# Chunkwise retention with a running K^T V state, plain fp32 loads and an instruction order written by hand, in a retention + gated FFN kernel

## The chip, the cores and the metric

The kernel runs on one core of a Trainium2 chip. The metric is the device time of one execution in microseconds (us), lower is better. TensorE (PE) multiplies matrices, PEld is its weight load, VectorE (DVE), ScalarE (ACT) and GpSimd (POOL) compute elementwise, SyncE (SP) issues DMAs. TensorE writes to PSUM, from which the others copy to SBUF.

## The reference

Retention is attention without softmax: scores are scaled, masked to the causal triangle and weighted by gamma^(i-j), one gamma per head. Its output goes through a sigmoid-gated FFN.

```python
batch, n_heads, seq, head_dim = (8, 8, 576, 64)
scores = scale * np.matmul(q, k.transpose(0, 1, 3, 2))
gamma = 1.0 - 2.0 ** (-5.0 - np.arange(H, dtype=np.float32))
Dmat = np.where(rel >= 0, gamma[:, None, None] ** rel[None, :, :], 0.0)
ret = np.matmul(scores * Dmat[None, :, :, :], v)
# x: ret as (4608 tokens, 512)
gate = 1.0 / (1.0 + np.exp(-(x @ w_gate)))     # w_gate, w_val: 512 x 1536
out = (gate * (x @ w_val)) @ w_out             # w_out: 1536 x 512
```

All inputs and the output are fp32 in memory; both kernels multiply in bf16. Since gamma^(i-j) = gamma^i gamma^(-j), both put one factor into q and the other into k.

## The kernel before

The work has two stages per batch. `attention_batch(b)` makes the 576 tokens of batch b for all eight heads, handled in four pairs of two heads (2 x 64 = 128 partitions). `ffn_window(w)` takes 512 tokens of the result, which lies transposed in `xT`, through the FFN. The main loop issues the loads of the next batch, then attention, then one FFN window; a ninth window ends the program.

Loads (`load_qkv`, lines 119 to 136, and `load_weights`, lines 103 and 106) are all issued by GpSimd and cast fp32 to bf16 on the way. They share eight completion semaphores in turn, so at most eight are on the way. The code asks for batch 0, then all weights, then batch 1. V goes into `vpad`, which holds each head's 64 columns in a 128-wide block of zeros, so that two heads accumulate into one 128-partition result.

Attention, by line:
- 149: transposes of Q and K, 40 a batch, into the PSUM tile `tr` (one buffer).
- 165, 168, 171: VectorE multiplies by the gamma tables on the way out to `qTpad` (zeros in the other head's half) and `kTp`.
- 192, 210: K^T Q for the causal blocks of the full 576 x 576 matrix, 12 matmuls a pair of heads, up to 512 columns wide, into `qk` (three PSUM banks) and `pv`.
- 221 to 235: five masked diagonal blocks on VectorE and four plain copies on whichever engine the framework picks, into `pt`.
- 241 to 262: the products with V, in two parts through one PSUM bank `pv` (one buffer), copied to `xT`.

The FFN window: 12 column blocks, each four matmuls with `wg_sb` (271) and four with `wv_sb` (280), a sigmoid on ScalarE (288) and a product on VectorE (290); then for four blocks of 128 tokens twelve matmuls with `wo_sb` (295), a copy (303) and a store from SyncE (305). Three PSUM buffers `ffn` serve all of it. The order on each engine is set by the framework's scheduler from these loops; it mixes attention of the next batch with the start of a window.

Of the kernel before, what the change touches and what calls it, by code (L numbers as in the profile page):

```python
# [9 lines left out]
FP32 = mybir.dt.float32  # L10
BF16 = mybir.dt.bfloat16
# [5 lines left out]
def kernel(  # L17
# [9 lines left out]
):  # L27
    nc = tc.nc
# [4 lines left out]
    P = 128  # L33

    NPAIR = H // 2
    NSC = (S + P - 1) // P
    SC_OFF = [0, 128, 256, 384, S - P]
    NJC = NSC
    JTAIL = (NSC - 1) * P
    WTAIL = S - JTAIL  # L40
    SPAD = S + WTAIL
    NKC = DM // P
    NFC = DFF // P
    scale = 1.0 / math.sqrt(D)

    consts = ctx.enter_context(tc.tile_pool(name="consts", bufs=1))
    wpool = ctx.enter_context(tc.tile_pool(name="wpool", bufs=1))
    bfpool = ctx.enter_context(tc.tile_pool(name="bfpool", bufs=2))
    pt_pool = ctx.enter_context(tc.tile_pool(name="pt", bufs=4))
    xt_pool = ctx.enter_context(tc.tile_pool(name="xt", bufs=1))  # L50
    gv_pool = ctx.enter_context(tc.tile_pool(name="gv", bufs=13))
# [3 lines left out]
    qk_psum = ctx.enter_context(tc.tile_pool(name="qk_psum", bufs=3, space=bass.MemoryType.PSUM))  # L55
    pv_psum = ctx.enter_context(tc.tile_pool(name="pv_psum", bufs=1, space=bass.MemoryType.PSUM))
    tr_psum = ctx.enter_context(tc.tile_pool(name="tr_psum", bufs=1, space=bass.MemoryType.PSUM))
    ffn_psum = ctx.enter_context(tc.tile_pool(name="ffn_psum", bufs=3, space=bass.MemoryType.PSUM))

    ident = consts.tile([P, P], BF16)  # L60
    make_identity(nc, ident)

    maskfull = consts.tile([P, S], BF16)
    nc.gpsimd.memset(maskfull, 1.0)
    nc.gpsimd.affine_select(
        out=maskfull, in_=maskfull, compare_op=ALU.is_ge, fill=0.0, base=0,
        pattern=[[1, S]], channel_multiplier=-1)

    srow_f = consts.tile([P, S], FP32)
    nc.gpsimd.iota(srow_f, pattern=[[1, S]], base=0, channel_multiplier=0,  # L70
                   allow_small_or_imprecise_dtypes=True)
    grq = consts.tile([P, H, S], BF16)
    gmk = consts.tile([P, NPAIR, S], BF16)
    ln_scale_bias = consts.tile([P, 1], FP32)
    nc.vector.memset(ln_scale_bias, math.log(scale))
    for h in range(H):
        lg = math.log(1.0 - 2.0 ** (-5.0 - h))
        nc.scalar.activation(out=grq[:, h, :], in_=srow_f, func=AF.Exp,
                             bias=ln_scale_bias, scale=lg)
    for m in range(NPAIR):  # L80
        for hh in range(2):
            lg = math.log(1.0 - 2.0 ** (-5.0 - (2 * m + hh)))
            p0 = hh * 64
            nc.scalar.activation(out=gmk[p0:p0 + 64, m, :],
                                 in_=srow_f[p0:p0 + 64, :],
                                 func=AF.Exp, bias=0.0, scale=-lg)

    qTpad = consts.tile([P, 2, H, S], BF16)
    kTp = consts.tile([P, 2, NPAIR, SPAD], BF16)
    vpad = consts.tile([P, 2, NJC, NPAIR, 2, P], BF16)  # L90
    nc.vector.memset(qTpad, 0.0)
    nc.scalar.memzero(kTp)
    nc.gpsimd.memset(vpad, 0.0)  # L93

    wg_sb = wpool.tile([P, NKC, DFF], BF16)
    wv_sb = wpool.tile([P, NKC, DFF], BF16)
    wo_sb = wpool.tile([P, NFC, DM], BF16)

    def load_weights():
        for (dst, src, nch) in ((wg_sb, moe_w_gate, NKC), (wv_sb, moe_w_val, NKC)):  # L100
            for c in range(nch):
                for p0 in range(0, DFF, 512):
                    nc.gpsimd.dma_start(out=dst[:, c, p0:p0 + 512],
                                        in_=src[c * P:(c + 1) * P, p0:p0 + 512])
        for c in range(NFC):
            nc.gpsimd.dma_start(out=wo_sb[:, c, :],
                                in_=moe_w_out[c * P:(c + 1) * P, :])

    xT = xt_pool.tile([P, NPAIR, NT], BF16)

    def load_qkv(b):
        ph = b % 2
        qb = bfpool.tile([P, NSC, H, D], BF16, tag="qb", name=f"qb{b}")
        kb = bfpool.tile([P, NSC, H, D], BF16, tag="kb", name=f"kb{b}")
        for sc in range(NSC):
            s0 = SC_OFF[sc]
            for (t_ap, dst) in ((q, qb), (k, kb)):
                for hw in range(2):
                    nc.gpsimd.dma_start(  # L119
                        out=dst[:, sc, 4 * hw:4 * hw + 4, :],  # L120
                        in_=t_ap[b, 4 * hw:4 * hw + 4, s0:s0 + P, :]
                        .rearrange("h p d -> p h d"))
        for sc in range(NSC):
            s0 = SC_OFF[sc]
            if sc == NSC - 1:
                nc.gpsimd.dma_start(
                    out=vpad[0:WTAIL, ph, sc, :, 0, 0:D],
                    in_=v[b, 0::2, JTAIL:S, :].rearrange("h p d -> p h d"))
                nc.gpsimd.dma_start(
                    out=vpad[0:WTAIL, ph, sc, :, 1, D:2 * D],  # L130
# [214 lines left out]
```

## Time and profile before

| | |
|---|---|
| median of 3 runs | 475.63 us (475.23 to 477.93) |
| the profiled execution (its span, first to last instruction) | 474.0 us |
| TensorE busy | 413.1 us, 87%, 2,470 matmuls recorded |
| VectorE busy | 212.5 us, 45% |
| ScalarE busy | 191.9 us, 40% |
| GpSimd busy | 206.1 us, 43% (most of it DMA issues) |
| DMA queues | GpSimd's: 127,808 packets; SyncE's: 5,184 |
| mean granted TensorE clock | 0.986 |

Busy time of an engine is the union of its instructions. Matmuls overlap, so their starts tell the pace. Some matmul records are missing (of the FFN's 1,296, the page has 1,255). In rows of stretches the columns are: stretch and length, busy time and count of each engine, granted clock, DMA share, GB/s written. In rows of groups: line, engine, operation, out<-in, count, busy us and mean ns, idle time before and what ended it.

### The profile page before, as it was taken

To read this page: it belongs to the slowest core of one execution; us is meant where nothing else is said; L and a number is where in the kernel's file an instruction comes from. 1 tells how busy PE (TensorE), PEld (TensorE's weight loads), DVE (VectorE), ACT (ScalarE), POOL (GpSimd) and SP (SyncE) were. 2 spreads that over 40 slices of the span, in tenths; PEclk is the share of its full clock that TensorE was granted. 3 is DMA by queue.
4 is the path that set the end of the run, shared out by engine and by line. 5 is a ranking of instruction groups with operands and counts; after the bars stand their busy time and mean duration, and the time that the engine had idled before them with its cause. 6 is when DMAs were issued, how large, how long until landed. Compare 5 with 4: busy or idle time off the path is not lost.

```text
span 474.0 us, 6814 instructions
## 1 busy us (share of the span) xinstructions
PE 413.1 (87%) x2470; PEld 217.1 (46%) x2512; DVE 212.5 (45%) x600; ACT 191.9 (40%) x433; POOL 206.1 (43%) x286
## 2 busy tenths in 40 slices
PE   0375799589999899899989998999899998999996
PEld 0133444355445544464445444644465445444442
DVE  3255241487417641674248333844195308441330
ACT  9225332055325532563246332733264326532331
POOL 9997899999407730575048602960000000000000
PEclk9999899789999999999999999999999999999999
DMA  0999999999719951797059703990200010001002
GB/s 0 78 86 182 190 117 124 138 86 91 46 46 101 72 36 44 83 74 51 22 91 88 51 1 96 90 67 2 89 2 1 0 66 24 2 0 61 30 0 89
DMA packets 133025, 29.81 MB, mean 63 GB/s; under 512 B 123776, under 2 KB 128384, under 8 KB 132992
## 3 DMA queue, kind: packets, MB, share of 16 engines
q0 software_dynamic: 127808, 19.94, 57.2%
q1 hardware_dynamic: 5184, 9.44, 5.2%
q8 instruction: 19, 0.31, 0.3%
q14 instruction: 14, 0.11, 0.1%
HBM read 39.85 MB, written 9.44 MB: 104 GB/s over the span
## 4 chain that ended last, share of the span: by engine, by line
PE 73%; DVE 9%; POOL 7%; ACT 5%; DMA 2%; issue 2%; ACTq 0%; DVEq 0%; POOLq 0%
PE op L295 20%; PE h L280 19%; PE h L271 17%; PE qk L192 6%; PE pv L254 4%; PE pv L241 3%; PE tr L149 3%; DVE qTpad L165 2%; DVE qTpad L168 2%; POOL vpad L93 2%; POOL kb L119 2%; POOL qb L119 1%; DVE kTp L171 1%; DMA wv_sb<-in_moe_w_val_dram 1%; ACT pt L232 1%
## 5 line engine op out<-in xcount | busy, mean ns | idle before, releaser
L290 DVE TENSOR_TENSOR gv<-g,h 128x512 bf16<-128x512 bf16 x108 | 74.2, 687 | 127.8 <-PE h L280 107.7
L280 PE MATMUL h<-xT,wv_sb 128*128 128x512 bf16 x426 | 113.6, 379 | 6.6 <-DMA wv_sb<-in_moe_w_val_dram 3.7
L271 PE MATMUL h<-xT,wg_sb 128*128 128x512 bf16 x405 | 111.8, 380 | 1.5 <-DMA wo_sb<-in_moe_w_out_dram 0.8
L119 POOL DMA_DIRECT2D qb<-in_q_dram x80 | 66.3, 918 | 96.2 <-PE tr L149 96.1
L288 ACT ACTIVATE g<-h 128x512 bf16<-128x512 f32 x108 | 63.7, 598 | 106.4 <-PE h L271 98.4
L295 PE MATMUL op<-wo_sb,gv 128*128 128x512 bf16 x424 | 94.3, 379 | 0.5
L192 PE MATMUL qk<-qTpad,kTp 128*128 128x320 bf16 (+3 forms) x319 | 64.7, 303 | 9.5 <-DVE qTpad L165 6.5
L280 PEld LDWEIGHTS <-wv_sb 128*128 128x128 bf16 x432 | 42.3, 98 | 54.8 <-DMA wv_sb<-in_moe_w_val_dram 4.5
L119 POOL DMA_DIRECT2D kb<-in_k_dram x80 | 66.7, 931 | 0.1
L295 PEld LDWEIGHTS <-gv 128*128 128x128 bf16 x432 | 42.3, 98 | 51.0
L271 PEld LDWEIGHTS <-wg_sb 128*128 128x128 bf16 x432 | 42.3, 98 | 46.1
L165 DVE TENSOR_TENSOR qTpad<-tr,grq 64x512 bf16<-64x512 bf16 (+1 forms) x40 | 15.5, 388 | 95.5 <-PE tr L149 95.4
L303 ACT COPY ob<-op 128x512 f32<-128x512 f32 x36 | 21.1, 585 | 80.2 <-PE op L295 80.2
L149 PE MATMUL tr<-ident,qb 128*128 128x128 bf16 x160 | 20.5, 237 | 31.3 <-DVE kTp L171 16.3
L232 ACT CAST pt<-qk 128x384 bf16<-128x384 f32 x55 | 26.4, 480 | 42.8 <-DVE pt L221 42.6
L192 PEld LDWEIGHTS <-kTp 128*128 128x128 bf16 x320 | 27.5, 100 | 24.5 <-issue 11.8
L133 POOL DMA_DIRECT2D vpad<-in_v_dram x32 | 30.4, 950 | 10.2 <-PE pv L254 10.2
L254 PE MATMUL pv<-pt,vpad 128*128 128x192 bf16 (+1 forms) x320 | 29.2, 238 | 5.2 <-ACT xT L249 3.6
L149 PEld LDWEIGHTS <-qb 128*128 128x128 bf16 x160 | 12.4, 104 | 45.5 <-issue 24.2
L136 POOL DMA_DIRECT2D vpad<-in_v_dram x32 | 30.7, 960 | 0.4 <-PE h L271 0.4
L254 PEld LDWEIGHTS <-vpad 128*128 128x128 bf16 x320 | 25.9, 99 | 10.5 <-issue 8.3
L241 PE MATMUL pv<-pt,vpad 128*128 128x384 bf16 (+2 forms) x192 | 29.5, 277 | 0.9 <-DVE pt L229 0.2
(44 smaller groups left out, 342.3 us busy)
## 6 DMA issues: line engine op xcount, KB each, us to landing
out_dram<-ob SPq DMA_DIRECT2D x36, 256.0 KB, 2.0
qb<-in_q_dram POOLq DMA_DIRECT2D x80, 64.0 KB, 3.2
kb<-in_k_dram POOLq DMA_DIRECT2D x80, 64.0 KB, 3.3
vpad<-in_v_dram POOLq DMA_DIRECT2D x64, 64.0 KB, 3.2
wg_sb<-in_moe_w_gate_dram POOLq DMA_DIRECT2D x12, 128.0 KB, 5.5
wv_sb<-in_moe_w_val_dram POOLq DMA_DIRECT2D x12, 128.0 KB, 4.9
wo_sb<-in_moe_w_out_dram POOLq DMA_DIRECT2D x12, 128.0 KB, 4.9
vpad<-in_v_dram POOLq DMA_DIRECT2D x16, 32.0 KB, 3.0
```

The costliest lines, as they stand in the source:

```text
L119: nc.gpsimd.dma_start(out=dst[:, sc, 4 * hw:4 * hw + 4, :], in_=t_ap[b, 4 * hw:4 * hw + 4, s0:s0 + P, :] .rearrange("h p d -> p h d"))
L136: nc.gpsimd.dma_start(out=vpad[:, ph, sc, :, 1, D:2 * D], in_=v[b, 1::2, s0:s0 + P, :].rearrange("h p d -> p h d"))
L149: nc.tensor.matmul(trp[:, idx, :], lhsT=src[:, sc, 2 * m:2 * m + 2, :], rhs=ident, is_transpose=True, start=(idx == 0), stop=(idx == 2 * N ...
L192: nc.tensor.matmul(bank[:, off:off + wi], lhsT=kTp[:, ph, m, lj:lj + P], rhs=qTpad[:, ph, 2 * m + hh, li:li + wi], start=start, stop=stop,)
L232: nc.any.tensor_copy(out=pt[:, 0, P:512], in_=bks1[hh][:, P:512])
L241: nc.tensor.matmul(pvp[:, jc * P:W1], lhsT=vpad[:, ph, jc, m, hh, :], rhs=pts[hh][:, jc, jc * P:W1], start=(n1 == 0), stop=(n1 == 5),)
L254: nc.tensor.matmul(pvp[:, lo - W1:S - W1], lhsT=vpad[:, ph, jc, m, hh, :], rhs=pts[hh][:, jc, lo:S], start=(n2 == 0), stop=(n2 == 9),)
L271: nc.tensor.matmul(h1, lhsT=wg_sb[:, kc, fc * P:(fc + 1) * P], rhs=xT[:, kc, n0:n0 + 512], start=(kc == 0), stop=(kc == NKC - 1),)
L280: nc.tensor.matmul(h2, lhsT=wv_sb[:, kc, fc * P:(fc + 1) * P], rhs=xT[:, kc, n0:n0 + 512], start=(kc == 0), stop=(kc == NKC - 1),)
L288: nc.scalar.activation(out=g, in_=h1, func=AF.Sigmoid)
L290: nc.vector.tensor_tensor(out=gv, in0=g, in1=h2, op=ALU.mult)
L295: nc.tensor.matmul(opp, lhsT=gvs[fc][:, nb * P:(nb + 1) * P], rhs=wo_sb[:, fc, :], start=(fc == 0), stop=(fc == NFC - 1),)
```

## The change

Attention is rewritten; the FFN keeps its matmuls.

- **Chunks with a state.** Each batch is cut into 5 chunks (four of 128 tokens, one of 64), 40 chunks in all. Within a chunk the causal product is formed in two halves of 64 keys, both heads of a pair at once, with K laid in diagonal blocks (`kbd`) and V too (`vbd`). What earlier chunks contribute comes from a 64 x 64 state K^T V per head, summed in one PSUM tile `st` over the batch, and copied with a mask to bf16 (`sb`) after each chunk.
- **Loads.** Q, K and V come as fp32 by SyncE's queue, one DMA each for a chunk (256 KB as fp32, 256 B per row), six chunks ahead. The gamma factors and casts are made on chip before the transposes (`cast`): in the first five chunks K on VectorE, Q on GpSimd, V on ScalarE; later all on GpSimd. Weights stay on GpSimd's queue, in 9 DMAs of 1 MB (as fp32) instead of 36. They too take the eight completion semaphores in turn, so the ninth waits for the first.
- **Order.** The framework's scheduler is off (`manual_schedule`), so each engine runs in the order of the code. Each chunk has four phases: t (transposes), qk, pv, st. The first four chunks run ahead of the FFN; then phases are laid between the FFN's units, each of four matmuls.
- Output copies and their stores go to ScalarE.

The diff, cut to its core:

```diff
+    ctx.enter_context(tc.manual_schedule())
+    STEPS = [(b, c) for b in range(B) for c in range(NC)]
+    def load(s):
...
+        for nm, src in (("k", k), ("q", q), ("v", v)):
+            t = ld_pool.tile([P, H, D], FP32, tag=nm + "32", name=f"{nm}32_{s}")
+            nc.sync.dma_start(out=t[0:n], in_=src[b, :, t0:t0 + n, :].rearrange("h p d -> p h d"))
...
+    LEAD_LOAD = 6
+    LEAD_CAST = 3
...
+    def load_weights():
+        for f0 in range(0, DFF, 512):
+            for dst, src in ((wg_sb, moe_w_gate), (wv_sb, moe_w_val)):
+                nc.gpsimd.dma_start(
+                    out=dst[:, :, f0:f0 + 512],
+                    in_=src[:, f0:f0 + 512].rearrange("(c p) f -> p c f", p=P))
...
+    def cast(s):
...
+        early = s < NC
+        eng = nc.vector if early else nc.gpsimd
+        eng.tensor_tensor(out=ks[0:n], in0=k32[0:n],
+                          in1=ktab[0:n, c, :].unsqueeze(2).to_broadcast([n, H, D]), op=ALU.mult)
+        nc.gpsimd.tensor_tensor(out=qs[0:n], in0=q32[0:n],
+                                in1=qtab[0:n, c, :].unsqueeze(2).to_broadcast([n, H, D]), op=ALU.mult)
...
+        copy(vn[0:n], v32[0:n])
+        for j in range(n // 64):
+            for hh in range(2):
+                copy(vb[hh * 64:hh * 64 + 64, j, :, hh * 64:hh * 64 + 64],
+                     v32[j * 64:j * 64 + 64, hh::2, :])
...
+    def phase_t(s):
...
+                nc.tensor.matmul(trp[:, i * M + m, 0:n], lhsT=src[0:n, 2 * m:2 * m + 2, :],
+                                 rhs=ident[0:n, 0:n], is_transpose=True,
...
+            nc.vector.tensor_copy(
+                out=kb[p0:p0 + 64, 0:nj, :, p0:p0 + 64].rearrange("p j m t -> p m j t"),
+                in_=trp[p0:p0 + 64, 0:M, 0:n].rearrange("p m (j t) -> p m j t", t=64))
...
+        nc.scalar.copy(out=qT[:, :, 0:n], in_=trp[:, M:2 * M, 0:n])
...
+    def phase_qk(s):
...
+                    nc.tensor.matmul(qkp[:, mm, 0:128], lhsT=kb[:, 0, m, :], rhs=qT[:, m, 0:128],
+                                     start=True, stop=True)
+                    nc.tensor.matmul(qkp[:, mm, 128:192], lhsT=kb[:, 1, m, :], rhs=qT[:, m, 64:128],
+                                     start=True, stop=True)
+                nc.vector.tensor_tensor(out=pt[:, 2 * g:2 * g + 2, :], in0=qkp[:, :, 0:192],
+                                        in1=tri.unsqueeze(1).to_broadcast([P, 2, 192]), op=ALU.mult)
...
+    def phase_pv(s):
...
+            if c > 0:
+                mm.append((state[s - 1][:, m, :], qT[:, m, 0:n], 0, n))
+            if n == P:
+                mm.append((vb[:, 0, m, :], pt[:, m, 0:128], 0, 128))
+                mm.append((vb[:, 1, m, :], pt[:, m, 128:192], 64, 128))
...
+        nc.scalar.copy(out=xT[:, :, t0:t0 + n], in_=pvp[:, :, 0:n])
...
+    def phase_st(s):
...
+            nc.tensor.matmul(stp[:, m, :], lhsT=ks[:, 2 * m:2 * m + 2, :], rhs=vn[:, 2 * m:2 * m + 2, :],
...
+    def phase_sv(s):
...
+        nc.vector.tensor_tensor(out=sb, in0=st_tiles[b],
+                                in1=bdm.unsqueeze(1).to_broadcast([P, M, P]), op=ALU.mult)
...
+    order = [("t", 0), ("qk", 0), ("st", 0)]
+    for s in range(NS):
+        if s + 1 < NS:
+            order.append(("t", s + 1))
+        order.append(("pv", s))
+        if s + 1 < NS:
+            order.append(("qk", s + 1))
+            order.append(("st", s + 1))
...
+        for u, _ in enumerate(ffn_units(t0, n)):
+            want = begin + min(todo, -(-todo * (u + 1) // (nu - 3)))
+            while at < want:
+                run_phase(*order[at])
+                at += 1
...
-    staged = load_qkv(0)
     load_weights()
-    for b in range(B):
-        staged_next = load_qkv(b + 1) if b + 1 < B else None
-        attention_batch(b, staged)
-        staged = staged_next
-        ffn_window(b)
-    ffn_window(B)
```

`run_phase`, at t of chunk s, first issues the load of chunk s + 6 and the casts of chunk s + 2.

How this stands on the engines, at the places that the prediction speaks of. GpSimd's start before, from the constants to the first loads of batch 0 (`qb`, `kb`):

```order
L65 AFFINE_SELECT maskfull<-maskfull 128x576
L70 IOTA srow_f 128x576
L93 MEMSET vpad 128x10240
L119 DMA qb_131<-in_q_dram 128x4x64 x2
L119 DMA kb_132<-in_k_dram 128x4x64 x2
```

GpSimd's start after, from the fifth of the nine weight DMAs (ahead of the first stand the constants and the Q scaling of chunks 0 and 1) to the first chunk that it casts alone, number 5; `qs`, `ks` are scaled Q and K of a chunk, `vn` its V:

```order
L134 DMA wg_sb<-in_moe_w_gate_dram 128x4x512
L134 DMA wv_sb<-in_moe_w_val_dram 128x4x512
L138 DMA wo_sb<-in_moe_w_out_dram 128x4x512 x3
L159 TENSOR_TENSOR qs_214<-q_2_107,qtab 128x512
L159 TENSOR_TENSOR qs_263<-q_3_113,qtab 128x512
L159 TENSOR_TENSOR qs_321<-q_4_119,qtab 64x512
L157 TENSOR_TENSOR ks_382<-k_5_123,ktab 128x512
L159 TENSOR_TENSOR qs_381<-q_5_125,qtab 128x512
L166 CAST vn_383<-v_5_127 128x512
```

The weights have moved ahead of most of the loads' consumers: the Q scaling of chunks 2 to 4 stands behind all nine weight DMAs.

ScalarE's rows before, from the gamma tables to the first copies of scores of batch 0:

```order
L78 ACTIVATE grq<-srow_f,ln_scale_bias 128x576 x8
L84 ACTIVATE gmk<-srow_f 64x576 x8
L232 CAST pt_0_0_291<-qk_0_0_0_292 128x384
L232 CAST pt_0_1_295<-qk_0_0_1_296 128x384
L233 CAST pt_0_0_291<-qk_0_0_0_293 128x64
```

ScalarE's rows after, from the gamma tables to the copies of the transposed Q (`qT`) of the first chunks and of the first result (`pv` to `xT`):

```order
L101 ACTIVATE qtab<-arg,lnscale 128x40
L164 CAST vn_181<-v_0_97 128x512
L164 CAST vbd_151<-v_0_97 64x4x64 x4
L164 CAST vn_191<-v_1_103 128x512
L164 CAST vbd_152<-v_1_103 64x4x64 x4
L164 CAST vn_216<-v_2_109 128x512
L164 CAST vbd_153<-v_2_109 64x4x64 x4
L198 COPY qT_235<-tr_224 128x512
L164 CAST vn_265<-v_3_115 128x512
L164 CAST vbd_154<-v_3_115 64x4x64 x4
L198 COPY qT_284<-tr_273 128x512
L245 CAST xT<-pv_286 128x4x128
```

The copy of chunk 0's Q stands behind the casts of V of chunk 2, that of chunk 1 behind those of chunk 3, and so on.

VectorE's rows before inside an FFN window (`gv` is the gate product; the window is the second):

```order
L290 TENSOR_TENSOR gv_9_1209<-g_9_1207,h_1_9_1202 128x512
L290 TENSOR_TENSOR gv_10_1223<-g_10_1221,h_1_10_1216 128x512
L290 TENSOR_TENSOR gv_11_1237<-g_11_1235,h_1_11_1230 128x512
L165 TENSOR_TENSOR qTpad<-tr_4_1383,grq 64x4x64
L168 TENSOR_TENSOR qTpad<-tr_4_1383,grq 64x4x64
L171 TENSOR_TENSOR kTp<-tr_4_1383,gmk 128x4x64
```

VectorE's rows after inside the first window, chunk 5 between the gate products (`kbd` from the transposes, `pt` the masked scores, `sb` the state):

```order
L315 TENSOR_TENSOR gv_1_513<-g_1_506,h_0_1_508 128x512
L194 COPY kbd_157<-tr_531 64x4x2x64 x2
L315 TENSOR_TENSOR gv_2_566<-g_2_549,h_0_2_561 128x512
L215 TENSOR_TENSOR pt_575<-qk_0_576,tri 128x384
L215 TENSOR_TENSOR pt_575<-qk_1_582,tri 128x384
L315 TENSOR_TENSOR gv_3_593<-g_3_573,h_0_3_588 128x512
L265 TENSOR_TENSOR sb_607<-st_602,bdm 128x512
L315 TENSOR_TENSOR gv_4_614<-g_4_600,h_0_4_609 128x512
```

Attention's work, which stood in a block after the gate products, is now spread between them, at most two operations at a time.

442 lines of the change are left out of this document (202 added, 240 removed).

## The prediction

> **What bounds the kernel now.** I read the busy shares first, then the busy time of stretches of the span, then single rows of the timeline. The page's two lines:
>
> ```profile
> span 474.0 us, 6814 instructions
> PE 413.1 (87%) x2470; PEld 217.1 (46%) x2512; DVE 212.5 (45%) x600; ACT 191.9 (40%) x433; POOL 206.1 (43%) x286
> ```
>
> TensorE is far ahead of the others, but its 87% is made of overlapping matmuls, so the stretches and the spacing of starts say more. The stretches are: before the first transpose, up to the first FFN matmul, first FFN window, second batch, and one settled batch.
>
> ```profile
> 0.00:14.40 14.40, 0.00 (x0) 0.00 (x0) 3.96 (x2) 13.51 (x17) 13.76 (x14) 1.00 0.09 6
> 14.40:41.20 26.80, 17.45 (x109) 9.13 (x111) 14.24 (x49) 7.93 (x23) 25.82 (x40) 1.00 1.33 103
> 41.20:85.00 43.80, 37.23 (x189) 18.37 (x192) 11.73 (x27) 14.52 (x29) 40.01 (x62) 0.96 1.38 152
> 85.00:145.00 60.00, 51.91 (x332) 29.04 (x335) 30.93 (x88) 21.67 (x51) 38.77 (x54) 0.91 0.98 79
> 194.30:243.80 49.50, 46.27 (x295) 24.81 (x298) 24.67 (x73) 20.81 (x51) 22.00 (x30) 1.00 0.67 60
> ```
>
> So 85 us pass before the first FFN window is done, the second batch costs 60 us, and from then on a batch costs 49.5 us. Rows of TensorE in settled batches, in order of time, and two of the chain of waits at the end:
>
> ```profile
> 193.87 0.38 PE L149 MATMUL tr<-ident,qb 128*128 128x128 bf16 x4 [0.61 <-DVE kTp L171]
> 194.09 0.39 PE L149 MATMUL tr<-ident,kb 128*128 128x128 bf16 x4
> 207.23 0.88 PE L254 MATMUL pv<-pt,vpad 128*128 128x192 bf16 x10
> 207.94 0.60 PE L192 MATMUL qk<-qTpad,kTp 128*128 128x320 bf16 x4
> 213.15 1.02 PE L280 MATMUL h<-xT,wv_sb 128*128 128x512 bf16 x4
> 214.01 1.03 PE L271 MATMUL h<-xT,wg_sb 128*128 128x512 bf16 x4
> 243.41 0.38 PE L149 MATMUL tr<-ident,qb 128*128 128x128 bf16 x4 [0.61 <-DVE kTp L171]
> 459.61 10.54 PE op L295 x48
> 470.21 0.58 ACT ob L303
> ```
>
> Starts, not durations, give the price of a matmul. Four of 512 columns take 214.01 - 213.15 = 0.86 us, 0.216 each. Four transposes of 128 columns take 0.22, 0.055 each. That is 0.42 ns a column plus about 1.3 ns. The ten of line 254 (eight of 192 columns, two of 64) take 0.71 us, which that line gives too (0.70), so a matmul of 64 columns costs 0.028 us. The same place of two batches lies 243.41 - 193.87 = 49.54 us apart. The FFN's 144 matmuls are 31.1 us of it. The batch's attention is 152 matmuls over 30,720 columns (counted from the code), 13.1 us. The remaining 5.3 us are waits inside attention, such as the 0.61 us for VectorE in two of these rows. After the last matmul (470.15) the span goes on for 3.8 us: a copy and a store.
>
> **TensorE's new work.** The FFN keeps its 1,296 matmuls: 1,296 x 0.216 = 279.9 us. A chunk of 128 tokens now has 8 transposes, 4 products with K, 4 state updates and 8 products with V or the state, 24 of 128 columns, and 8 of 64: 24 x 0.055 + 8 x 0.028 = 1.54 us. The first chunk of a batch has four fewer of 128 (no state yet), 1.32; the last, 64 tokens wide, has 20 of 64 columns, 0.56. A batch is 1.32 + 3 x 1.54 + 0.56 = 6.5 us instead of 13.1, and eight are 52.1. Chunks 0 to 3 and the transposes of chunk 4 (6.2 us) come before the first FFN matmul, so 45.9 us follow it.
>
> The Trainium skill (TensorE: Matmul & The Clock Gate, section Back-to-back issue gap) says that in a stream of weight load and matmul pairs 128 columns settle at about 81 ns a matmul. The transposes above, each with its own weight load, start 55 ns apart, so the trace disagrees. By the page the 636 such matmuls after the start would add 636 x 0.026 = 17 us.
>
> **Stalls between phases.** The phases t, pv, qk and st of a chunk are laid between FFN units of four matmuls (0.86 us), about two units apart. The cover is thus 1.7 us for what VectorE and ScalarE must do between two phases. Their rows:
>
> ```profile
> L290 DVE TENSOR_TENSOR gv<-g,h 128x512 bf16<-128x512 bf16 x108 | 74.2, 687 | 127.8 <-PE h L280 107.7 <-ACT g L288 19.0 <-PE h L271 1.0
> L288 ACT ACTIVATE g<-h 128x512 bf16<-128x512 f32 x108 | 63.7, 598 | 106.4 <-PE h L271 98.4 <-PE h L280 7.9
> L303 ACT COPY ob<-op 128x512 f32<-128x512 f32 x36 | 21.1, 585 | 80.2 <-PE op L295 80.2
> L227 DVE TENSOR_TENSOR pt<-qk,maskfull 128x192 bf16<-128x192 f32 x64 | 22.2, 348 | 0.0
> L223 DVE TENSOR_TENSOR pt<-qk,maskfull 128x128 bf16<-128x128 f32 x64 | 18.3, 286 | 0.8 <-PE qk L192 0.4
> L165 DVE TENSOR_TENSOR qTpad<-tr,grq 64x512 bf16<-64x512 bf16 x32 | 13.3, 415 | 80.0 <-PE tr L149 79.9
> ```
>
> The new mask multiply has 384 columns: from 286 and 348 ns about 1 ns a column, so 534 ns, two per chunk. The K copies are like line 165 (2 x 415 ns), the state's multiply like line 290 (687). With 13.5 gate products VectorE has about 21 us of work in a batch's 41.5; ScalarE, with 13.5 sigmoids, 4.5 output copies and nine copies of about 585 ns, about 16, and the output's DMA issue moves to its queue. Neither is a bound, but their order matters. An FFN buffer (three of them) must be free two units after it was filled, 1.73 us; with both mask multiplies ahead in VectorE's queue its product is done after 2 x 0.53 + 0.69 = 1.76 us, plus a handoff. I take 0.2 us lost in each of the 28 full chunks after the start, 5.6 us. The bounds are 0 (settled FFN rows show no gap) and 5.3 us a batch as now, 38 us over the 7.2 batches left.
>
> **Loads and casts.** A load becomes 1,024 packets of 256 B on SyncE's queue, three loads a chunk. GpSimd issues only weights, in 9 large DMAs, and casts from chunk 5 on. Rows (stretches first):
>
> ```profile
> 40.00:45.00 5.00, 3.03 (x26) 1.71 (x23) 3.30 (x13) 3.64 (x11) 2.91 (x7) 1.00 1.23 195
> 45.00:50.00 5.00, 2.88 (x17) 2.24 (x19) 0.75 (x3) 0.50 (x2) 4.38 (x9) 0.74 1.20 189
> 50.00:55.00 5.00, 3.66 (x26) 2.13 (x25) 0.62 (x3) 1.85 (x5) 4.02 (x9) 0.92 1.20 188
> 62.00:63.50 1.50, 1.50 (x9) 0.67 (x8) 0.69 (x1) 0.37 (x2) 1.50 (x4) 1.00 2.04 130
> 242.49 0.33 SPq L305 DMA_DIRECT2D out_dram<-ob  x1
> out_dram<-ob SPq DMA_DIRECT2D x36, 256.0 KB, 2.0
> 33.44 5.58 POOL L103 DMA_DIRECT2D wg_sb<-in_moe_w_gate_dram  x10
> L65 POOL TENSOR_SCALAR_AFFINE_SELECT maskfull<-maskfull 128x576 bf16<-128x576 bf16 x1 | 0.7, 665 | 0.0
> L93 POOL MEMSET vpad<- 128x10240 bf16 x1 | 8.6, 8627 | 0.0
> ```
>
> At 62 us a backlog of 128 B packets moves at 130 GB/s, 1.02 packets a ns: I take 1.0 us a load, since the packet count is the nearest likeness. Upwards, the store's issue on SyncE (0.33 us for 128 packets of 2 KB) would be 2.6 us if it grew with packets. The weights moved at 188 to 195 GB/s of bf16, so their 4.72 MB take about 25 us.
>
> **First FFN matmul.** Chunk 4's transposes stand ahead of it, so 4.5 chunks, 13.5 loads, must land: 13.5 us plus 2 for landing, 16 us alone. The weights join at about 9.5 us (GpSimd first scales Q of chunks 0 and 1, the latter after the fifth load). If all 25 us of them went first, it would be 41. I take the middle, 28. Then V of chunk 4 is cast on ScalarE ahead of older copies (1.2 us), and three chunks follow one another at about 2.5 us (transposes 0.6, copy 0.6, product 0.3, masks 1.1): 9 us. The first FFN matmul is at 37 us, bounds 25 and 50. The lowered clock at a cold start (0.74 and 0.92 in two rows above) costs (0.26 + 0.08) x 5 = 1.7 us.
>
> **The sum.** 37 + 279.9 + 45.9 + 5.6 + 1.7 + 3.8 = 373.9 us. The profiled execution stands 1.6 us under the median of the runs (474.0 and 475.63), so 375.5: I say 376. Of the 100 us saved, 53 come from columns ((13.1 - 6.5) x 8), about 37 from waits (4.5 us a batch, and 10 more in the second batch), and the rest from the first window.
>
> **Rivals.**
> *Waits stay.* Chunks hand over as slowly as now, 5.3 us a batch: 376 + 38 - 6 = 408. For it: one transpose buffer and one for PV remain. Against: hand-laid FFN units lie between all phases.
> *Weight loads show.* A load lasts 98 ns, longer than a short matmul; if the 43 ns beyond 55 were not hidden, 636 x 0.043 = 27 us, 403. The 55 ns spacing speaks against it.
> *Weights hold GpSimd.* The ninth weight DMA waits for the first, and the Q scaling of chunks 2 to 4 is queued behind it. In the row at 33 us ten issues went 0.53 us apart without a wait, so I count no hold. If GpSimd were held until most of the 25 us had moved, under sharing until about 45, the FFN would start at 55: 394.
> *GpSimd becomes the bound, slower than before.* Per chunk it makes two multiplies of 512 columns, one copy of 512 and four of 256. From its two rows (0.84 ns a column, 0.18 us fixed) a copy is 0.61 or 0.40; the multiplies, with two inputs, between that and twice it. So 3.4 to 4.6 us a chunk, against 41.5/4.5 = 9.2 that TensorE leaves. It decides beyond 9.2. The 31.5 chunks after the fourth begin near 38 us, and 43 us follow the last cast, so 12.5 us a chunk reach 475 and 14 make 522. No arithmetic of this form ran there before.
> *Loads become the bound.* Past 41.5/13.5 = 3.1 us a load; at 3.5, 108 loads and the end give about 425.
>
> The Trainium skill (GPSIMD Engine Reference, section 3.1 Elementwise) gives about 2.6 cycles an element at 1.2 GHz for two inputs. As an estimate from that page a multiply is 1.1 us, which leaves the sum as it is; no run here shows it yet.
>
> **How the numbers follow.** Forecast 0.70; waits stay 0.12; weight loads show 0.03; GpSimd held 0.07; GpSimd bound 0.05; loads bound 0.03. The forecast's own ends: start at 25 and no stalls, 376 - 12 - 5.6 = 358; start at 50 and 15 us of stalls, 376 + 13 + 9.4 = 398. The range is 360 to 408: it leaves out a sliver below, half of "waits stay" and the two bounds. A measurement of this kernel can tell about 0.5% from no change. Faster 0.92, the same 0.02 (the bounds at their thresholds), slower 0.06.
>
> **What would show it.** Right: op rows of neighbouring windows about 37 us apart on average (31.1 plus 5.8), transposes still at 0.055 us, no gap over 0.5 us on TensorE past the first window, GpSimd's casts under 5 us a chunk, first FFN matmul between 25 and 50 us. Wrong: TensorE waiting on casts or loads, or gaps at every phase.

## The result and the profile after

The changed kernel takes 389.81 us (median of 4 runs, 387.2 to 389.84), the kernel before 476.4 beside it (4 runs, 475.23 to 477.93): a ratio of 0.8172 with a 95% interval of 0.8142 to 0.8203. The forecast was 376, range 360 to 408. The profiled execution took 389.82 us, its span 388.1. Its first two lines:

```profile
span 388.1 us, 6403 instructions
PE 341.4 (88%) x2403; PEld 186.0 (48%) x2448; DVE 166.7 (43%) x310; ACT 137.9 (36%) x251; POOL 158.2 (41%) x263
```

TensorE is as far ahead as before, with 72 us less busy time. The stretches, cut as in the prediction: the first transposes, up to the first FFN matmul, the first window, the second, a settled one.

```profile
0.00:12.30 12.30, 1.22 (x8) 0.69 (x8) 5.29 (x18) 6.00 (x13) 9.62 (x24) 1.00 1.10 186
12.30:53.10 40.80, 11.95 (x124) 11.32 (x125) 11.01 (x23) 10.27 (x23) 14.93 (x22) 1.00 1.22 201
53.10:81.10 28.00, 27.61 (x192) 14.77 (x196) 15.26 (x28) 11.23 (x19) 18.80 (x31) 1.00 1.19 203
81.10:118.10 37.00, 36.74 (x268) 19.78 (x271) 17.52 (x32) 14.54 (x26) 17.38 (x30) 1.00 0.78 161
155.40:192.40 37.00, 36.68 (x267) 19.76 (x271) 17.55 (x32) 14.44 (x26) 18.18 (x32) 1.00 0.48 118
```

From 53.1 us on TensorE is busy for all but 0.3 to 0.4 us of each window. Nearly all that went other than forecast lies in the second row: 40.8 us, of which TensorE works 12. TensorE's rows at the same place of two neighbouring windows:

```profile
154.99 0.39 PE L187 MATMUL tr<-ident,ks 128*128 128x128 bf16 x4
155.21 0.39 PE L187 MATMUL tr<-ident,qs 128*128 128x128 bf16 x4
155.43 1.03 PE L321 MATMUL op<-wo_sb,gv 128*128 128x512 bf16 x3
...
192.37 0.81 PE L321 MATMUL op<-wo_sb,gv 128*128 128x512 bf16 x3
```

Four transposes still start 0.22 us apart, and the op rows of two neighbouring windows lie 36.94 us apart where one place of two batches lay 49.54 (each has one FFN window; the attention in it is that of 512 tokens now, of 576 before). The engines that copy, by groups:

```profile
L159 POOL TENSOR_TENSOR qs<-q,qtab 128x512 bf16<-128x512 f32 (+1 forms) x40 | 41.7, 1042 | 22.7 <-DMA q<-in_q_dram 22.4
L215 DVE TENSOR_TENSOR pt<-qk,tri 128x384 bf16<-128x384 f32 x64 | 32.7, 552 | 75.5 <-PE qk L213 75.5
L166 POOL CAST vbd<-v 64x256 bf16<-64x256 f32 x126 | 50.2, 399 | 54.8 <-PE pv L244 50.8
L166 POOL CAST vn<-v 128x512 bf16<-128x512 f32 (+1 forms) x35 | 21.3, 608 | 0.6 <-DMA v<-in_v_dram 0.6
L138 POOL DMA_DIRECT2D wo_sb<-in_moe_w_out_dram x3 | 2.3, 775 | 0.7 <-DMA wg_sb<-in_moe_w_gate_dram 0.7
```

**Where the start goes.** The casts of chunks 3 and 4 in order of time, each started by its load, and the steps of TensorE after them (the bracket holds the idle time before and what ended it):

```profile
20.39 0.69 DVE L157 TENSOR_TENSOR ks<-k,ktab 128x512 bf16<-128x512 f32 x1 [1.76 <-DMA k<-in_k_dram]
27.04 1.04 POOL L159 TENSOR_TENSOR qs<-q,qtab 128x512 bf16<-128x512 f32 x1 [8.51 <-DMA q<-in_q_dram]
33.62 0.62 ACT L164 CAST vn<-v 128x512 bf16<-128x512 f32 x1 [17.25 <-DMA v<-in_v_dram]
40.45 1.04 POOL L159 TENSOR_TENSOR qs<-q,qtab 64x512 bf16<-64x512 f32 x1 [12.37 <-DMA q<-in_q_dram]
43.69 0.62 ACT L164 CAST vn<-v 64x512 bf16<-64x512 f32 x1 [6.81 <-DMA v<-in_v_dram]
45.70 0.26 PE L211 MATMUL qk<-qT,kbd 128*128 128x128 bf16 x1 [6.12 <-ACT qT L198]
49.44 0.27 PE L211 MATMUL qk<-qT,kbd 128*128 128x128 bf16 x1 [0.59 <-ACT qT L198]
53.11 0.59 PE L306 MATMUL h<-xT,wg_sb 128*128 128x512 bf16 x1 [0.73 <-ACT xT L245]
```

The three loads of chunk 3 land 6.6 us apart, those of the half-size chunk 4 3.2 us. Before the weights moved it was 1.2 us a load: V of chunks 0, 1 and 2 started its cast at 6.42, 10.05 and 13.59 us, three loads apart. The DMA view of three stretches, 5 to 10, 20 to 25 and 43.2 to 44.5 us (packets, MB, share of 16 engines; q1 is SyncE's queue, q0 GpSimd's), shows why; the last row is the issue of one load on SyncE:

```profile
q1 hardware_dynamic: 4328, 1.09, 138.8%
...
q0 software_dynamic: 776, 0.78, 91.4%
q1 hardware_dynamic: 776, 0.20, 29.8%
...
q1 hardware_dynamic: 1357, 0.34, 132.1%
...
7.29 1.14 SPq L78 DMA_DIRECT2D q<-in_q_dram  x1
```

While both queues have work, they move the same number of packets, though a weight packet holds 1 KB and a load's 256 B. The loads drop from 4,328 packets to 776, a fifth; the weights move at 156 GB/s (0.78 MB in 5 us) where they had 188 to 195 in the kernel before, so they lose only about a fifth. The loads crawl until the last weight is in, at 43.4 us. The 1.2 us of a load without weights may be the pace of SyncE's issues, 1.14 us each: behind the last weight, where loads had queued up, 1,357 packets go in 1.3 us, 1.0 us a load.

### The profile page after: what moved, and what is told of

Its sections match the earlier page's. It is cut to its first block, busy times and chain, and to the rows that moved or that the text cites. A ratio compares the mean times of both kernels' runs of the same rounds, so it can differ in the third digit from the quotient of the medians.

```text
span 388.1 us, 6403 instructions
## 1 busy us (share of the span) xinstructions
PE 341.4 (88%) x2403; PEld 186.0 (48%) x2448; DVE 166.7 (43%) x310; ACT 137.9 (36%) x251; POOL 158.2 (41%) x263
## 4 chain that ended last, share of the span: by engine, by line
PE 85%; SPq 6%; DMA 4%; issue 1%; ACT 1%; DVE 0%; ACTq 0%
PE h L306 48%; PE op L321 24%; SPq L78 6%; PE pv L244 4%; DMA v<-in_v_dram 4%; PE tr L187 4%; PE qk L211 2%; PE st L256 2%; PE qk L213 1%; ACT qT L198 0%; PE qk L220 0%; ACT vbd L164 0%; DVE pt L215 0%; DVE kbd L194 0%; ACT ob L326 0%
## 5 line engine op out<-in xcount | busy, mean ns | idle before, releaser
L166 POOL CAST vbd<-v 64x256 bf16<-64x256 f32 x126 | 50.2, 399 | 54.8 <-PE pv L244 50.8
L157 POOL TENSOR_TENSOR ks<-k,ktab 128x512 bf16<-128x512 f32 (+1 forms) x35 | 36.4, 1041 | 76.1 <-issue 57.9
L215 DVE TENSOR_TENSOR pt<-qk,tri 128x384 bf16<-128x384 f32 x64 | 32.7, 552 | 75.5 <-PE qk L213 75.5
L306 PEld LDWEIGHTS <-wg_sb 128*128 128x128 bf16 x432 | 40.9, 99 | 45.3 <-issue 2.5
L159 POOL TENSOR_TENSOR qs<-q,qtab 128x512 bf16<-128x512 f32 (+1 forms) x40 | 41.7, 1042 | 22.7 <-DMA q<-in_q_dram 22.4
L211 PE MATMUL qk<-qT,kbd 128*128 128x128 bf16 x128 | 16.3, 228 | 32.5 <-ACT qT L198 32.4
L198 ACT COPY qT<-tr 128x512 bf16<-128x512 bf16 (+1 forms) x40 | 21.7, 543 | 51.6 <-DVE kbd L194 47.0
L194 DVE COPY kbd<-tr 64x512 bf16<-64x512 bf16 (+1 forms) x80 | 31.5, 394 | 15.5 <-PE tr L187 14.3
L265 DVE TENSOR_TENSOR sb<-st,bdm 128x512 bf16<-128x512 f32 x32 | 22.0, 687 | 11.0 <-PE st L256 11.0
L244 PE MATMUL pv<-pt,vbd 128*128 128x64 bf16 (+1 forms) x288 | 24.9, 213 | 0.0
L245 ACT CAST xT<-pv 128x512 bf16<-128x512 f32 (+1 forms) x40 | 21.8, 544 | 6.9 <-PE pv L244 6.9
L166 POOL CAST vn<-v 128x512 bf16<-128x512 f32 (+1 forms) x35 | 21.3, 608 | 0.6 <-DMA v<-in_v_dram 0.6
```

Of the source, the lines that this page charges most:

```text
L157: eng.tensor_tensor(out=ks[0:n], in0=k32[0:n], in1=ktab[0:n, c, :].unsqueeze(2).to_broadcast([n, H, D]), op=ALU.mult)
L159: nc.gpsimd.tensor_tensor(out=qs[0:n], in0=q32[0:n], in1=qtab[0:n, c, :].unsqueeze(2).to_broadcast([n, H, D]), op=ALU.mult)
L166: nc.gpsimd.tensor_copy(out=o, in_=i)
L194: nc.vector.tensor_copy(out=kb[p0:p0 + 64, 0:nj, :, p0:p0 + 64].rearrange("p j m t -> p m j t"), in_=trp[p0:p0 + 64, 0:M, 0:n].rearrange(" ...
L211: nc.tensor.matmul(qkp[:, mm, 0:128], lhsT=kb[:, 0, m, :], rhs=qT[:, m, 0:128], start=True, stop=True)
L215: nc.vector.tensor_tensor(out=pt[:, 2 * g:2 * g + 2, :], in0=qkp[:, :, 0:192], in1=tri.unsqueeze(1).to_broadcast([P, 2, 192]), op=ALU.mult)
```

## The experiments

The theory behind all of them: packets of the two queues take turns one for one, so what sets the first FFN matmul is when the weights are issued and how many packets they are; from the first FFN matmul on TensorE's columns are the bound, because the code lays FFN units between the phases. Ratios below are to the kernel before; that of the kernel after is 0.8172 (0.8142 to 0.8203).

**Weights later.** All nine DMAs are issued after chunk 4's Q scaling.

```diff
+            if s == 2:
+                load_weights()
             phase_t(s)
...
-    load_weights()
     end = upto(last_step(WINDOWS[0][0] + WINDOWS[0][1]))
```

> All nine weight DMAs are issued by GpSimd after the Q scaling of chunk 4 instead of before that of chunk 2; nothing else changes. Theory (packets of SyncE's loads and of GpSimd's weights take turns one for one on the DMA engines, so the loads crawl at 6.6 us each until the weights are in): the first fifteen loads go alone at 1.2 us each, V of chunk 4 lands at about 19 us instead of 43.6, the first FFN matmul stands at 28 to 30 us instead of 53.1, the weights (started at about 18 us, 3.35 us apart while loads run beside them) are just in time, and the time is 365 to 368 us instead of 389.8. Rival (the sum of bytes sets the start, so what the loads gain the weights lose): the FFN then waits for its weights or its chunks inside the first window, the second window starts no earlier than 118 us less 5, and the time is 385 or more.

Measured: 375.0 us, ratio 0.7879 (0.7853 to 0.7905), so 14.8 us below the kernel after. V of chunk 4 lands before 21.2 us, and:

```profile
17.52 0.62 ACT L164 CAST vn<-v 128x512 bf16<-128x512 f32 x1 [1.11 <-DMA v<-in_v_dram]
32.07 1.86 PE L308 MATMUL h<-xT,wg_sb 128*128 128x512 bf16 x4 [1.70 <-ACT xT L245]
53.51 1.04 POOL L159 TENSOR_TENSOR qs<-q,qtab 128x512 bf16<-128x512 f32 x1 [5.58 <-DMA q<-in_q_dram]
54.60 0.40 PE L187 MATMUL tr<-ident,qs 128*128 128x128 bf16 x4 [3.43 <-POOL qs L159]
```

The first FFN matmul comes 21 us earlier. It misses the 28 to 30 expected: with early loads V of chunk 4 ends no wait any more, and from V of chunk 3 (17.5 us) it is four steps from chunk to chunk, 14.5 us. (The copy behind that V's casts waits another 0.45 us for chunk 1's transposes, so this V is only about the last to come.) Then about 5 us are given back by the profiled spans (372.1 and 388.1): the loads of chunk 7 now crawl beside the output weights, and TensorE waits 3.4 us for its Q. The time lies between the ranges of theory and rival; the theory holds for the start, the rival for a part of what it is worth.

**A third of the weights later.** Only the output weights move behind chunk 4's Q scaling.

```diff
+
+    def load_wo():
         for c0 in range(0, NFC, 4):
             nc.gpsimd.dma_start(
                 out=wo_sb[:, c0:c0 + 4, :],
...
+            if s == 2:
+                load_wo()
             phase_t(s)
```

> Only the three DMAs of the output weights, a third of the weight bytes, move behind the Q scaling of chunk 4. Theory (turns one for one): the mixing ends when six weight DMAs are in, about 10 us earlier (three DMAs 3.35 us apart); after that loads land 1.2 us apart, so V of chunk 4 lands at about 36 us, the first FFN matmul at 45 to 46 us, and the time is about 382 us. Rival (the first FFN matmul is set by the chain of casts and copies, not by the loads): 388 to 391, the first FFN matmul within 1 us of 53.

Measured: 386.04 us, ratio 0.8109 (0.8087 to 0.813); 3.8 us gained, not 8. Rows of the start, in order of time:

```profile
35.87 0.62 ACT L166 CAST vn<-v 128x512 bf16<-128x512 f32 x1 [19.11 <-DMA v<-in_v_dram]
38.70 0.27 PE L213 MATMUL qk<-qT,kbd 128*128 128x128 bf16 x1 [19.17 <-ACT qT L200]
39.16 0.62 ACT L166 CAST vn<-v 64x512 bf16<-64x512 f32 x1
40.52 1.08 POOL L159 TENSOR_TENSOR ks<-k,ktab 128x512 bf16<-128x512 f32 x1
40.76 2.40 DVE L159 TENSOR_TENSOR ks<-k,ktab 64x512 bf16<-64x512 f32 x1
44.68 0.22 PE L213 MATMUL qk<-qT,kbd 128*128 128x128 bf16 x1 [2.83 <-ACT qT L200]
51.87 1.44 PE L310 MATMUL h<-xT,wg_sb 128*128 128x512 bf16 x3 [0.73 <-ACT xT L247]
```

V of chunk 4 was there before 39.2 us (its cast waited for nothing), but V of chunk 3 came only at 35.9, since nearly all loads up to it had still gone beside the first six weights, and the chain from there takes 16 us (1.7 of them in the multiply at 40.76 us, which took 2.40 us where it took 0.68 in the kernel after). So there are two bounds on the first FFN matmul: V of chunk 4 plus 9.4 us, and V of chunk 3 plus 14.5 to 16. My expectation had only the first.

**Smaller weight packets.** The gate and value weights in 12 DMAs of 256 columns; Q of chunks 2 to 4 on VectorE.

```diff
-        for f0 in range(0, DFF, 512):
+        for f0 in range(0, DFF, 256):
...
-                    out=dst[:, :, f0:f0 + 512],
-                    in_=src[:, f0:f0 + 512].rearrange("(c p) f -> p c f", p=P))
+                    out=dst[:, :, f0:f0 + 256],
+                    in_=src[:, f0:f0 + 256].rearrange("(c p) f -> p c f", p=P))
...
-        nc.gpsimd.tensor_tensor(out=qs[0:n], in0=q32[0:n],
+        qeng = nc.vector if 2 <= s < NC else nc.gpsimd
+        qeng.tensor_tensor(out=qs[0:n], in0=q32[0:n],
```

> The gate and value weights come in twelve DMAs of 256 columns (packets of 512 B as bf16) instead of six of 512 columns (1 KB); the bytes and their order stay. Since more DMAs wait for a semaphore lane, the Q scaling of chunks 2 to 4 goes to VectorE (about 1 us each). Theory (turns are taken packet for packet, whatever their size): beside smaller packets a load's 1,024 packets need less time, 4 to 5 us instead of 6.6, V of chunk 4 lands at 35 to 38 us, the first FFN matmul at 45 to 48, the time is about 382 to 385 us; the gate and value weights land later than before by the same token. Rival (the two queues share bytes, or the weights go first): load spacing stays 6.6 us, V of chunk 4 stays at 43 to 44 us and the time at 388 to 391.

Measured: 377.35 us, ratio 0.7928 (0.791 to 0.7946). The queues in 20 to 25 us, when 512 B packets move, and in 40 to 45 us, when the output weights' 1 KB packets do:

```profile
q0 software_dynamic: 1226, 0.61, 88.4%
q1 hardware_dynamic: 1228, 0.31, 46.7%
...
q0 software_dynamic: 786, 0.78, 91.8%
q1 hardware_dynamic: 782, 0.20, 29.8%
```

and the casts that wait for V of chunk 3, V of chunk 4, and Q and V of chunk 5:

```profile
25.08 0.62 ACT L165 CAST vn<-v 128x512 bf16<-128x512 f32 x1 [8.64 <-DMA v<-in_v_dram]
31.59 0.62 ACT L165 CAST vn<-v 64x512 bf16<-64x512 f32 x1 [3.24 <-DMA v<-in_v_dram]
...
42.03 1.04 POOL L160 TENSOR_TENSOR qs<-q,qtab 128x512 bf16<-128x512 f32 x1 [5.10 <-DMA q<-in_q_dram]
48.61 0.61 POOL L167 CAST vn<-v 128x512 bf16<-128x512 f32 x1 [5.54 <-DMA v<-in_v_dram]
```

One and a half loads (chunk 4) take 6.5 us beside 512 B packets, 4.3 a load; a load takes 6.6 again beside 1 KB packets. The counts stay equal in both. Turns by count are thus shown, and sharing by bytes is refuted. The gain, 12.5 us, is more than the 5 to 8 expected, because V of chunk 4 came at 31.6, not 35 to 38; the first FFN matmul stands at 41.0, again 9.4 us behind it.

**The order.** All phases of a window stand in one block behind its first unit; and, apart from that, the framework's scheduler instead of the order of the code.

```diff
-            want = begin + min(todo, -(-todo * (u + 1) // (nu - 3)))
+            want = end if u >= 1 else begin
```

> All phases that the first code lays between the units of a window are put in one block behind the window's first unit; the matmuls, casts and loads stay. Theory (the order by hand hides the handoffs between TensorE and the engines that copy): without FFN units between them the phases of a chunk follow one another at about 2 us more a chunk (copy 0.6, masks 0.55 to 1.1, result copy 0.6, one transpose and one product buffer), so 28 chunks of 128 tokens and the short ones give 450 to 460 us, with waits for VectorE and ScalarE on the rows of transposes and products. Rival (the order is worth little, the saving comes from fewer columns): 390 to 400 us.

```diff
-    ctx.enter_context(tc.manual_schedule())
```

> The kernel after without manual_schedule: the framework's scheduler sets the order on each engine, chunks, casts and loads stay as written. Theory (half of the saving comes from the order): waits between attention's phases come back to some 4 to 5 us a batch, 410 to 425 us. Rival (columns alone): within 5 us of 390. It tells less than phases_in_a_block if the scheduler happens to leave the order of the code.

Measured: 456.74 us for the block (one run), as the theory said; 386.27 for the framework's order (one run), where I expected 410 to 425. The block's busy times, rows of one chunk after another in a settled window, and the group that waits:

```profile
PE 371.7 (82%) x2448; PEld 204.0 (45%) x2448; DVE 163.9 (36%) x310; ACT 137.7 (30%) x251; POOL 156.2 (34%) x263
...
156.76 0.27 PE L211 MATMUL qk<-qT,kbd 128*128 128x128 bf16 x1 [1.07 <-ACT qT L198]
...
157.78 0.63 PE L187 MATMUL tr<-ident,ks 128*128 128x128 bf16 x4
158.20 0.63 PE L187 MATMUL tr<-ident,qs 128*128 128x128 bf16 x4
...
160.50 0.22 PE L211 MATMUL qk<-qT,kbd 128*128 128x128 bf16 x1 [0.59 <-ACT qT L198]
...
L211 PE MATMUL qk<-qT,kbd 128*128 128x128 bf16 x128 | 17.6, 239 | 62.6 <-ACT qT L198 62.6
```

In the kernel after that group waited 32.4 us, all of it before the first FFN matmul; here 30 us more, mostly 0.6 to 1.7 us a time. Between op rows lie 45.3 us on average instead of 37.2. Waits are only about half of the loss: of the 67 us over the kernel after TensorE stands idle for some 37 (455.0 - 371.7 us against 388.1 - 341.4) and is busy for some 30 with the same matmuls (371.7 against 341.4). Behind the waits four transposes start 0.42 us apart instead of 0.22, and the granted clock is 0.89 to 0.96 in seven of the eight windows up to the last-but-one op row, where it stood at 1.00. So 67 of the 87 us that the change brought hang on phases that stand apart. They don't hang on `manual_schedule`: without it TensorE's order differs only within the first 200 of 2,448 matmuls (by their weight loads), then the scheduler keeps the code's. That run can therefore not say what a different order costs, as its expectation allowed.

**Casts one chunk ahead at the start**, instead of two, so that ScalarE's copy of a transposed Q no longer stands behind the V casts of a chunk two ahead.

```diff
-            while done["cast"] < min(NS, s + LEAD_CAST):
+            while done["cast"] < min(NS, s + (2 if s < 4 else LEAD_CAST)):
```

> The kernel after with one edit: in the first four chunks casts run one chunk ahead of the transposes instead of two. Theory (V of chunk 4 lands at 43.6 us whatever the casts do, and the chain from there is 9.5 us, three steps): the chain loses about one step of 3.6 us, the first FFN matmul is at 49 to 50 us and the time at 386 us. Rival (the chain does not matter, only the loads): the same as the kernel after, 389 to 390. A second rival (the chain starts at V of chunk 3, 33.6 us, and its 15 us decide): no gain below 48.6 us, which can't be told from the theory here.

Measured: 386.21 us, ratio 0.8099 (0.8069 to 0.8129), as expected; the first FFN matmul at 50.72 instead of 49 to 50. The chain counts, but only for 2.4 us at the start and 1.2 in the first window.

**Looking for the best version.** Four further kernels combine these edits, and a fifth takes bytes away.

```diff
             if s == 2:
                 load_weights()
+            if s == 5:
+                load_wo()
```

> As weights_after_chunk4 (375.0 us), but the three output-weight DMAs go behind the casts of chunk 7. There TensorE waited 3.4 us at 54.6 us for Q of chunk 7, whose load landed at 53.5 us beside the output weights. Theory (loads crawl as long as any weight packets are queued): the six gate and value DMAs are in at about 41 us, the loads of chunk 7 land by about 45 to 47 us, that wait goes, the output weights start at about 48 us and are just in time for the first op row, which stands at about 60 instead of 64 us; 370 to 372 us. Rival (bytes decide, so the wait only moves): the first op row waits for the output weights or a later chunk for its loads, and the time stays 374 to 376.

Measured: 376.06 us, ratio 0.7881 (0.7854 to 0.7908): the rival, though the first op row comes at 59.5 us, as the theory said. The wait for Q of chunk 7 is gone; instead TensorE waits 2.2 us for the output weights (at 64.1 us), and the second op row comes 43.8 us after the first instead of 37.

With the casts one chunk ahead as well; the gate and value weights move with them, so that they still stand behind chunk 4's Q scaling:

```diff
-            while done["cast"] < min(NS, s + LEAD_CAST):
+            while done["cast"] < min(NS, s + (2 if s < 4 else LEAD_CAST)):
...
-            if s == 2:
+            if s == 3:
                 load_weights()
```

> As weights_late_wo_later, and in the first four chunks the casts run one chunk ahead of the transposes instead of two, so ScalarE's copies of the transposed Q no longer stand behind the V casts of a chunk two ahead. Theory (a chain of four chunk steps of 3.6 us from V of chunk 3 sets the first FFN matmul once the loads are early, 14.5 us from 17.5 to 32.1 there): one or two steps less after the last V cast, the first FFN matmul at 26 to 29 us, and about 366 to 369 us if weights and loads still come in time. Rival (the weights or the loads of the first window are the bound by then): the first FFN matmul or the first op row waits for a DMA, and the time is within 1 us of weights_late_wo_later.

Measured: 373.88 us, ratio 0.7833 (0.7804 to 0.7862), the lowest median of a complete kernel here, though its interval overlaps that of weights_after_chunk4. It lies between theory and rival: 3.5 us of gain at the start became 2.2 at the end. The same edit to the casts on two kernels shown above, weights_after_chunk4 (where `load_weights` moves to s == 3 too) and half_weight_packets:

```diff
-            while done["cast"] < min(NS, s + LEAD_CAST):
+            while done["cast"] < min(NS, s + (2 if s < 4 else LEAD_CAST)):
```

> As weights_after_chunk4 (375.0 us; first FFN matmul at 32.1), with the casts of the first four chunks one chunk ahead instead of two; the output weights stay with the others. Theory (by now the DMA engines' work up to the second window is the bound: about 27 loads at 1.2 us, nine weight DMAs at 3.1, less some 3 us that mixing saves, plus 4 us before the first landing, 61 us): the first FFN matmul comes at 28 to 29 us, but TensorE waits longer for chunk 7, and the time is 373 to 375. Rival (the start still counts in full): 371.5 or less.

> As half_weight_packets (377.35 us; first FFN matmul at 41.0), and in the first four chunks the casts run one chunk ahead of the transposes instead of two, as in lead2. Theory (the first window there had no loss, and the chain from the last V cast is one step shorter): the first FFN matmul at 37 to 38 us, 373.5 to 375 us. Rival (the transfers of the first windows are the bound by now): what is gained at the start is lost to waits for loads in the first two windows, 376 to 378.

Measured: 376.46 us, ratio 0.7903 (0.7877 to 0.7928), and 378.85, ratio 0.795 (0.7915 to 0.7984). Neither gains on the kernel that it starts from, 375.0 and 377.35. The first FFN matmul comes at 29.2 and 39.6 us, and the next windows lose it: in the one 44.0 us pass from the first op row to the second (38.0 in the kernel that it starts from), in the other 31.8 instead of 28 us up to the first op row. In the first kernel neither range holds: the time is 1.5 us above the theory's, and the wait for chunk 7 is hardly longer (3.6 us against 3.4); the loss lies in the second window, where TensorE waits 5.0 us in three waits from 76.6 us on. In the second it is the rival in kind, 0.9 us above its range.

Then the output weights cut to a third:

```diff
-        for c0 in range(0, NFC, 4):
+        for c0 in range(0, 4, 4):
...
-                nc.tensor.matmul(opp, lhsT=gvs[fc][:, nb * P:(nb + 1) * P], rhs=wo_sb[:, fc, :],
+                nc.tensor.matmul(opp, lhsT=gvs[fc][:, nb * P:(nb + 1) * P], rhs=wo_sb[:, fc % 4, :],
```

> As late_wo_later_lead2 (373.9 us), with one output-weight DMA instead of three; all twelve blocks of the output product then use the four blocks that are loaded, so two thirds of the output weights are left out, while TensorE's work stays. Theory (the DMA engines' work is the bound of the first two windows): 1,024 packets of 1 KB less on 16 engines at 96 ns are 6.1 us, and 5 to 7 us of the 6.8 us that are lost there go: 367 to 369 us. Rival (the loss is in the chain of casts and copies): 373 to 374.5.

Measured: 367.12 us, ratio 0.7713 (0.7697 to 0.7729). The stretch from the first op row to the second, first with all output weights, then with a third:

```profile
58.61:102.22 43.61, 39.56 (x267) 20.65 (x270) 17.51 (x32) 14.53 (x26) 24.89 (x42) 0.92 1.23 224
```

```profile
59.13:96.06 36.93, 36.93 (x271) 19.70 (x269) 17.52 (x32) 14.53 (x26) 23.27 (x38) 1.00 1.11 219
```

6.8 us go where 6.1 were counted from the packets. That the two lie so close is partly luck: in the stretch above TensorE stands idle for 4.1 us (43.61 - 39.56), and the other 2.6 us are the same matmuls at a lower granted clock (39.56 busy against 36.93). So once the first FFN matmul is near 30 us, the bytes of the first two windows are the bound, in every order tried here.

**Columns.** Each product of K and Q is made twice into the same place (the repeated lines stand one level deeper in the code, and the chunk of 64 tokens is treated the same way).

```diff
+                    for rep in range(2):
                     nc.tensor.matmul(qkp[:, mm, 0:128], lhsT=kb[:, 0, m, :], rhs=qT[:, m, 0:128],
                                      start=True, stop=True)
                     nc.tensor.matmul(qkp[:, mm, 128:192], lhsT=kb[:, 1, m, :], rhs=qT[:, m, 64:128],
                                      start=True, stop=True)
```

> The kernel after, with each product of K and Q made twice into the same place (the second overwrites the first with the same values); nothing else changes. Theory (from the first FFN matmul on, TensorE's columns are the bound and nothing else waits): a chunk of 128 tokens has four more matmuls of 128 columns and four of 64, 4 x 0.055 + 4 x 0.028 = 0.33 us, 28 of them after the start make 9.3 us, the 64-token chunks 0.9 more, and three steps of the start 1.0: 400 to 401 us. Rival (VectorE, ScalarE or the loads set the pace and TensorE has slack between the phases): under 395.

Measured: 398.64 us, ratio 0.837 (0.8352 to 0.8388), 8.8 us over the kernel after by medians, 10.7 by the two profiled spans (398.8 and 388.1; runs of each kernel scatter by about 2 us). Between the first and the last op row it is 301.6 instead of 292.3 us, 9.3 more. That is the counted price: TensorE has no slack in which they could hide. The median lies 1.4 us below the theory's 400 to 401 and well above the rival's 395.

## Why the prediction was right, and which term was off

By its own sum, for the profiled execution: forecast 37 + 279.9 + 45.9 + 5.6 + 1.7 + 3.8 = 373.9; measured 53.1 up to the first FFN matmul, 330.8 from there to the end of the last matmul (forecast 333.1), 4.2 behind it, 388.1. The time stayed inside the range because the range was wide. One of the prediction's own signs failed: the first FFN matmul came at 53.1 us, not between 25 and 50, and up to there TensorE waited on loads, which it had named as a sign of being wrong; its other signs held.

- **Bound and new work: right.** TensorE's columns set the time from 53.1 us on, at 0.22 us for four transposes. Doubling a product cost its columns. The Trainium skill's 81 ns for such a matmul (TensorE: Matmul & The Clock Gate, section Back-to-back issue gap) isn't seen here either: 55 ns.
- **Stalls: bounds right, value too high.** Seven op-row spacings average 37.19 us ((341.43 - 81.12) / 7) where 36.9 was bare work. That is 2.0 us over some 25 full chunks, about 0.08 us a chunk, not 0.2. The block experiment shows what the cover is worth: 67 us, with the lower clock that the waits there bring.
- **Loads and casts alone: right.** A load took 1.2 us (taken 1.0, which is what a backlog of loads shows above); GpSimd's chunk is 2 x 1.04 + 0.61 + 4 x 0.40 = 4.3 us (forecast 3.4 to 4.6); the mask multiply 552 ns (534). The Trainium skill's rule of about 2.6 cycles an element (GPSIMD Engine Reference, section 3.1), 1.1 us as an estimate, agrees with 1.04.
- **First FFN matmul: the term that was mis-sized.** The step was "If all 25 us of them went first, it would be 41. I take the middle, 28." V of chunk 4 landed at 43.6 us, past even that bound: 16 us too late, more than the whole error of 14.2 us, since the other terms gave some back. The middle supposed that loads and weights share; they share packets, so the weights take 33 us (9.9 to 43.4) instead of 25 and the loads a fifth of their rate meanwhile. The chain behind it came out right only in its sum, which is luck: 9 forecast from 1.2 us and three steps of 2.5, 9.4 measured in 2.0 (43.69 to 45.70 us) and two steps of 3.7 (to 49.44 and 53.11). The rival that GpSimd is held named a time near the result (394) for a wrong reason: it was held 0.7 us.
- **Cold clock: small.** The first twelve FFN matmuls and four short products of chunk 4 among them took 58.38 - 53.11 = 5.3 us instead of 2.7 (12 x 0.216 + 4 x 0.028), so 2.6 us were lost where 1.7 was set. The profile writes a granted clock of 1.00 there, but its trace has no clock record before 58.3 us. The run with doubled products has one for the same place, and there the granted clock is 0.50. The rows of the kernel after, and then that stretch of the run with doubled products:

```profile
55.00 1.90 PE L306 MATMUL h<-xT,wv_sb 128*128 128x512 bf16 x4
56.69 1.85 PE L306 MATMUL h<-xT,wg_sb 128*128 128x512 bf16 x4
58.38 1.03 PE L306 MATMUL h<-xT,wv_sb 128*128 128x512 bf16 x4
```

```profile
54.30:57.70 3.40, 3.40 (x16) 1.44 (x16) 0.42 (x1) 1.82 (x2) 3.28 (x5) 0.50 1.07 229
```

- **A count.** The prediction's 636 matmuls of 128 columns after the start are 644 (28 x 24 less 4 for each of 7 first chunks); no term of the sum uses them.
- **Rivals.** "Waits stay" needed phases without cover, which the order doesn't leave. "GpSimd becomes the bound" stood at 4.3 of 9.2 us a chunk. "Loads become the bound" is false for settled windows, and true for the first two once the start is early.

What stays open: whether the last few us above 367 can be had with all weights. No order tried has a median below 373.9.

## What to carry to other kernels

When a prologue's small-row loads and bulk weights go through two queues at once, count packets, not bytes: the queue with the small packets gets the short end until the other is empty, so issue the bulk after the loads that the first result needs, or in smaller packets. Then look at what is late next, since the bytes are only moved: here 21 us of earlier start became 15. Interleaving phases with independent matmuls is what made the chunked form pay here: with the same phases in a block it gained 4% instead of 18%.

## What the runs showed of the hardware

- Two queues with work on the DMA engines take turns packet for packet: 776 and 776 in 5 us at 1 KB against 256 B, 1,226 and 1,228 at 512 B against 256 B. The Trainium skill (DMA: Bandwidth & Descriptors, section Queues, rings and completion order) says that an engine goes round between queues by whole packets, each of some 9 to 17 descriptors; the equal counts agree with turns that don't look at size, and a larger group on one side only isn't seen.
- By bytes written, loads alone moved 218 GB/s, a backlog of loads 261 (0.34 MB in 1.3 us), loads and weights together 195. The loads fell from 218 to 40 GB/s (0.20 MB in 5 us), so most of the harm lies in who waits, not in lost bandwidth.
- The first matmuls after a wait ran at half pace for 5 us (0.42 us at 512 columns); where the trace has a clock record for the same place, in the run with doubled products, the granted clock is 0.50. The Trainium skill (TensorE: Matmul & The Clock Gate, section Wait — 56ns, not 53.3ns?) gives 426.7 ns for 512 columns on a cold array, which agrees.
- A multiply of K on VectorE took 2.40 us instead of 0.68 while GpSimd multiplied K and Q of the next chunk (40.76 us in the second experiment). The Trainium skill (GPSIMD Engine Reference, section 1. Specifications) says that GpSimd shares its port to SBUF with VectorE's operations that have two inputs there; that fits, but no run here separates it from other causes.
